# Loads of a tuned attention and feed-forward kernel handed from SyncE to GpSimd

## The chip, the cores and the metric

One core of one Trainium2 chip. The metric is the time of one execution on the device in microseconds (us). Engines: TensorE (PE, its weight loads PEld), VectorE (DVE), ScalarE (ACT), GpSimd (POOL), SyncE (SP, its DMA queue SPq).

Kernels are compared only within the same rounds. With one core there is no other to compare with: a run counts as slow when it is over 1.5% above the fastest run of its kernel in its call.

## The reference

Cut to what matters: a linear attention with decay, computed in blocks along the sequence, then a feed-forward layer with the gate h·cos(h).

```python
# q, k, v: (4, 8, 768, 64) f32; lam: (8,); w_in: (512, 2048); w_out: (2048, 512)
for b in range(nb):                          # blocks of the sequence
    intra = (q_b @ k_b^T * Dmask) @ v_b      # per batch and head
    inter = (q_b * lam_pow) @ kv_state
    out_b = intra + inter
    kv_state = lam_block * kv_state + (k_b * rev_pow)^T @ v_b
x = out.transpose(0, 2, 1, 3).reshape(3072, 512)
h = x @ w_in
return (h * cos(h)) @ w_out
```

## The kernel before

The kernel takes the 3072 tokens as 24 blocks of 128. For each block from number 4 on, q, k and v (256 KB each, f32) are loaded from memory in pieces of 256 bytes, as each head's 64 numbers of one token lie apart.

```python
def start_load(o, x, deps):
    i = nc.sync.dma_start(out=o, in_=x)
    ...
def add_load(n, prio, deps=()):
    b, s0 = n // NB, (n % NB) * P
    for j, (name, src) in enumerate((("q_f", q), ("k_f", k), ("v_f", v))):
        def emit(name=name, src=src):
            t = loads.tile([P, H, D], F32, tag=name, name=name)      # 4 buffers of each
            live[name, n] = t
            return start_load(t, src[b, :, s0:s0 + P, :].transpose([1, 0, 2]), deps)
        issue, load_t[name, n] = dma("SP", 1.2, 0.45, emit, prio + 0.1 * j, deps, get=name)
        issue_t[name, n] = issue
```

GpSimd scales q, casts k and scales v to bf16 (three "preparations"); each frees a load buffer. From block 8 on, q and k are then transposed by a DMA that SyncE issues, and TensorE computes the scores from the result:

```python
a = pl.add("DVE" if n == 0 else "POOL", ..., prep_q, ...)
b = pl.add("ACT" if early else "POOL", 0.61, [load_t["k_f", n], a], prep_k, ...)
d = pl.add("POOL", 1.05, [load_t["v_f", n]], prep_v, ...)
for name, t in (("q_f", a), ("k_f", b), ("v_f", d)):
    issue_t[name, n].frees = [t]
...
if n >= DMA_FROM:                                                # 8
    first_out, T[n] = dma("SP", 1.2, 1.3, transposes_dma, ..., [a, b], get="qkT", ordered=False)
    if n + LAG < NBLK:
        issue_t["q_f", n + LAG].deps.append(first_out)           # loads of n + 2 after transpose n
```

`pl` is a planner that runs before the kernel is built. It gives every task an engine and a **reckoned** duration (the last number but the priority above: 0.45 us for an issue on SyncE, 1.05 for a multiply on GpSimd), plays the whole program through, and fixes the order of instructions on each engine from that. On the chip this order is static: if a task takes longer than was reckoned, the engines behind it wait; they do not take something else first.

Of the kernel before, what the change touches and what calls it, by code (L numbers as in the profile page):

```python
# [10 lines left out]
F32 = mybir.dt.float32  # L11
# [5 lines left out]
QK = 4  # L17
THIRD = 1
SPANS = 2
LAG = 2  # L20
ATT = 1.1
TILES = [4, 2, 3, 4, 4, 4, 3]
# [77 lines left out]
def kernel(  # L100
# [10 lines left out]
    nc = tc.nc  # L111
    B, H, S, D = q.shape
    P = 128
    NB = S // P
    NBLK = B * NB
    NP = H // 2
    DM = H * D
# [93 lines left out]
    def dma(queue, us, issue_us, emit, prio, deps=(), get=None, ordered=True):  # L211
        t = pl.add(queue, issue_us, list(deps) + [last_issue.get(queue) if ordered else None], emit, prio, get=get)
        if ordered:
            last_issue[queue] = t
        d = pl.add("DMA", us, [t], None, prio, lat=1.9)
        d.issue = t
        return t, d

    def start_load(o, x, deps):
        i = nc.sync.dma_start(out=o, in_=x)  # L220
        for d in deps:
            tc.add_manual_dep(i.ins, getattr(d, "issue", d).ins.ins.name, mybir.DependencyInfo(
                mybir.DependencyClass.Sync, mybir.DependencyReason.DATA), reason="order of loads")
        return i
# [9 lines left out]
# [3 lines that stand above are left out]
            def emit(name=name, src=src):  # L237
                t = loads.tile([P, H, D], F32, tag=name, name=name)
                live[name, n] = t
                return start_load(t, src[b, :, s0:s0 + P, :].transpose([1, 0, 2]), deps)  # L240
            issue, load_t[name, n] = dma("SP", 1.2, 0.45, emit, prio + 0.1 * j, deps, get=name)
            issue_t[name, n] = issue

    w_t = {}
# [20 lines left out]
    def add_attention(n):  # L265
# [43 lines left out]
        if n >= DMA_FROM:  # L309
            first_out, T[n] = dma("SP", 1.2, 1.3, transposes_dma, n - LAG + 1.5, [a, b], get="qkT", ordered=False)  # L310
            T[n].lat = 3.0
            ready = [T[n]]
            if n + LAG < NBLK:
                issue_t["q_f", n + LAG].deps.append(first_out)
        else:
            Tq = pl.add("PE", MM(P, 4), [a], lambda: transposes(0), pa(-0.05), get="ps_t")
            T[n] = pl.add("PE", MM(P, 4), [b, Tq], lambda: transposes(1), pa(0.0))
            sides = [slice(0, 1), slice(1, 2)] if early else [slice(0, 2)]
            ready = []
            for x in sides:  # L320
                ready.append(pl.add("DVE", 0.42 if early else 0.7, [T[n] if x.stop == 2 else Tq] + ready,
                                    partial(transposes_out, x), pa(0.0), get=None if ready else "qkT"))
            Tq.frees = [ready[-1]]
            first_out = ready[0]
# [235 lines left out]
    def add_ffn(i):  # L560
        nb, n0 = TILES[i], first[i]
        cols = nb * P
        gate = {}


        third = "ps_f" if i == 0 else "ps_t" if i >= THIRD else "ps_h"

        def bank_of(f):
            return third if f % 3 == 1 else "ps_h"

        for f in range(KF):
            pr = begins[i] + f * unit[i] / KF

            def hidden(f=f):
                t = bank(bank_of(f), [P, 4 * P], F32)
                for kd in range(KD):
                    ins = nc.tensor.matmul(t[:, :cols], lhsT=w_in_sb[:, kd, f * P:(f + 1) * P],  # L577
                                           rhs=live["xT", i][:, kd, :cols], start=(kd == 0), stop=(kd == KD - 1))
                live["h", i, f] = t
                return ins  # L580

            def cosine(f=f):
                c = work.tile([P, 4 * P], F32, tag="cos", name="cos")
                nc.scalar.activation(c[:, :cols], live["h", i, f][:, :cols], AF.Sin, bias=halfpi)  # L584
                live["c", i, f] = c

            def gated(f=f):
                if ("g", i) not in live:
                    live["g", i] = work.tile([P, KF, 4 * P], BF16, tag="g", name="g")
                nc.vector.tensor_mul(live["g", i][:, f, :cols], live.pop(("h", i, f))[:, :cols],  # L590
                                     live.pop(("c", i, f))[:, :cols])

            h = pl.add("PE", MM(cols, 4), [Vo[n] for n in range(n0, n0 + nb)] + [w_t["in", f * WCH // KF]],
                       hidden, pr, get=bank_of(f))
            a = pl.add("ACT", 0.26 + cols * 0.000833, [h], cosine, pr, get="cos")
            d = pl.add("DVE", 0.16 + cols * 0.00104, [a] + ([o_last[i - 2]] if i >= 2 else []), gated, pr)
            h.frees = [d]
            a.frees = [d]
            gate[f] = d
            h_last[i] = hid_t[i, f] = h  # L600
        nxt = unit[i + 1] if i + 1 < len(unit) else unit[i]
        U4 = 4
        for j in range(nb):
            last = n0 + j == NBLK - 1
            tag = ("ps_s", "ps_o", "ps_f", "ps_o")[(nb - 1 - j) % 4] if i == len(TILES) - 1 else "ps_f"

            pieces = [slice(0, DM // 2), slice(DM // 2, DM)] if last else [slice(0, DM)]
            evacs, stores = [], []
            store = None
            for piece, part in enumerate(pieces):  # L610
                width = part.stop - part.start
                for f0 in range(0, KF, U4):
                    pr = begins[i + 1] + (j + f0 / KF) * nxt / nb + piece

                    def project(j=j, f0=f0, tag=tag, piece=piece, part=part):
                        if f0 == 0 and piece == 0:
                            live["f", i, j] = ([bank("ps_s", [P, 2, DM], F32)[:, x, :width] for x in range(2)]
                                               if tag == "ps_s" else [bank(tag, [P, DM], F32)])
                        for f in range(f0, f0 + U4):
                            nc.tensor.matmul(live["f", i, j][piece], lhsT=live["g", i][:, f, j * P:(j + 1) * P],  # L620
                                             rhs=w_out_sb[:, f, part], start=(f == 0), stop=(f == KF - 1))

                    t = pl.add("PE", MM(width, U4), [gate[f] for f in range(f0, f0 + U4)] + [w_t["out", f0 * WCH // KF], store],
                               project, pr, get=tag if f0 == 0 and piece == 0 else None)
                    if f0 == 0 and piece == 0:
                        head = t
                    store = t
                o_last[i] = store

                def project_out(eng, j=j, i=i, piece=piece, width=width):  # L630
                    o = live["o_sb", i, j, piece] = work.tile([P, DM], F32, tag="o_sb", bufs=BUFS["o_sb"], name="o_sb")
                    (nc.scalar.copy if eng == "ACT" else nc.vector.tensor_copy)(o[:, :width], live["f", i, j][piece])  # L632

                def store_out(eng, j=j, piece=piece, part=part, width=width):
                    r0 = (n0 + j) * P
                    if n0 + j < 2 * SPANS:
                        for s, h in enumerate(halves):
                            nc.sync.dma_start(out=out[r0 + s:r0 + P:2, :], in_=live["o_sb", i, j, piece][h])
                        return
                    (nc.scalar if eng == "ACT" else nc.sync).dma_start(  # L640
                        out=out[r0:r0 + P, part], in_=live["o_sb", i, j, piece][:, :width])

                eng, queue = ("DVE", "SP") if last and piece == 0 else ("ACT", "ACT" if last else "SP")
                e = pl.add(eng, 0.12 + width / 1060.0, [store], partial(project_out, eng), begins[i + 1] + (j + 1) * nxt / nb,
                           get="o_sb")
                d = dma(queue, 0.7, 0.4, partial(store_out, queue), n0 + j + 8, [e], ordered=False)[1]
                e.frees = [d]
                evacs.append(e)
            head.frees = evacs

    kept = []
    for j, (name, x) in enumerate((("q", 0), ("k", 0), ("q", 1), ("k", 1), ("v", 0), ("v", 1))):
# [23 lines left out]
    idle_ps = bank("ps_h", [P, 4 * P], F32)  # L676

    def keep_awake(us, at):
        for _ in range(int(us / (4 * P / (1200.0 if at < 5.0 else 2400.0) + 0.0025))):
            nc.tensor.matmul(idle_ps, lhsT=ident, rhs=blank, start=True, stop=True)  # L680

    now = 1.6
    for t in pl.order():
# [35 lines left out]
```

## Time and profile before

| | before |
|---|---|
| time, median of the runs first given | 218.74 us (218.53 to 222.54, 3 runs) |
| span of the profiled run, granted clock | 217.3 us, 0.998 |
| TensorE busy | 95% |
| TensorE waiting for transposed q and k | 1.9 us, once |
| GpSimd busy | 66.2 us (30%) |
| transposes, issue to landing, median | 4.1 us |

Two more parts of the page are needed for the comparison: the slices of GpSimd and of the clock granted to TensorE (each digit is one fortieth of the span, in tenths), and the DMA queues (packets, MB, share of the 16 engines' time; the first is SyncE's, the second GpSimd's).

```profile
POOL 4594003786344545454444441300000000000000
PEclk9999999999999999999999999999999999999999
...
q1 hardware_dynamic: 89200, 29.24, 58.8%
q0 software_dynamic: 4224, 4.19, 11.8%
```

GpSimd is about 45% busy while the loads run, and the clock is full throughout. GpSimd issues only the eight weight loads: 4224 packets, 528 each.

### The profile page before, as it was taken

Reading aid. Unit: us, or ns where it says so; the run is one execution under the profiler, and the core shown is the slowest. Engines: PE = TensorE matmul, PEld = TensorE weight load, DVE = VectorE, ACT = ScalarE, POOL = GpSimd, SP = SyncE. Lnnn points to the kernel's source line nnn. Section 1 sums busy time; section 2 is a strip of 40 time slices with the busy share of each in tenths; the row PEclk is TensorE's granted clock in tenths of the full one; section 3 lists DMA queues with packets and bytes.
Section 4 is the critical chain, followed back from the end, with each engine's and each line's share of the span. In section 5 each row is a group of like instructions: output and inputs, shape, how many; then the busy total and the mean of one; then the engine's idle time right before and its main releaser. Section 6 shows DMA issues by size and latency. Waiting matters only on the chain.

```text
span 217.3 us, 4365 instructions
## 1 busy us (share of the span) xinstructions
PE 206.5 (95%) x1731; PEld 107.9 (50%) x1731; DVE 122.3 (56%) x217; ACT 106.7 (49%) x182; POOL 66.2 (30%) x85
## 2 busy tenths in 40 slices
PE   7797999999996999999999999999999999999993
PEld 2454444557664555454554445455454445555452
DVE  2694776456778677767765574674546334343200
ACT  5782775125664566464545435435444454445320
POOL 4594003786344545454444441300000000000000
PEclk9999999999999999999999999999999999999999
DMA  5999999999899999999899997201001101111112
GB/s 146 347 226 206 194 206 228 238 251 238 190 202 208 224 181 268 183 240 250 180 262 223 210 243 196 69 28 51 39 9 48 51 0 48 48 51 48 48 74 72
DMA packets 93588, 33.84 MB, mean 156 GB/s; under 512 B 80128, under 2 KB 90624, under 8 KB 93568
## 3 DMA queue, kind: packets, MB, share of 16 engines
q1 hardware_dynamic: 89200, 29.24, 58.8%
q0 software_dynamic: 4224, 4.19, 11.8%
q8 instruction: 13, 0.21, 0.4%
q10 hardware_dynamic: 144, 0.13, 0.2%
q14 instruction: 7, 0.06, 0.1%
HBM read 27.27 MB, written 6.29 MB: 154 GB/s over the span
## 4 chain that ended last, share of the span: by engine, by line
PE 89%; DMA 3%; DVE 3%; ACT 2%; issue 1%; POOL 1%; ACTq 0%
PE ps_f L620 36%; PE ps_h L577 26%; PE ps_t L577 10%; PE ps_s L331 3%; PE ps_o L356 3%; PE ps_o L360 2%; PE ps_f L577 2%; DMA qkT<-qk 2%; PE ps_s L620 2%; PE ps_o L620 2%; DVE s_m_sp L469 2%; DMA lam_bc<-in_lam_dram 1%; PE ps_h L680 1%; PE ps_kv L344 1%; POOL q_sp L432 1%
## 5 line engine op out<-in xcount | busy, mean ns | idle before, releaser
L620 PE MATMUL ps_f<-w_out_sb,g 128*128 128x512 bf16 x352 | 88.7, 379 | 0.3 <-ACT o_sb L632 0.2
L590 DVE TENSOR_TENSOR g<-ps_h,cos 128x512 bf16<-128x512 f32 (+2 forms) x77 | 47.2, 614 | 46.2 <-ACT cos L584 45.6
L584 ACT ACTIVATE cos<-ps_h,halfpi 128x512 f32<-128x512 f32 (+2 forms) x77 | 48.2, 626 | 49.4 <-PE ps_h L577 47.4
L577 PE MATMUL ps_h<-xT,w_in_sb 128*128 128x512 bf16 (+2 forms) x308 | 68.0, 349 | 0.0
L577 PEld LDWEIGHTS <-w_in_sb 128*128 128x128 bf16 x448 | 42.9, 98 | 41.4 <-issue 0.7
L620 PEld LDWEIGHTS <-g 128*128 128x128 bf16 x400 | 38.0, 98 | 39.6 <-issue 1.3
L274 POOL TENSOR_TENSOR qk<-q_f,q_scale 128x512 bf16<-128x512 f32 x20 | 20.8, 1042 | 51.8 <-DMA q_f<-in_q_dram 38.2
L584 ACT ACTIVATE cos<-ps_t,halfpi 128x512 f32<-128x512 f32 (+2 forms) x30 | 18.5, 616 | 20.6 <-PE ps_t L577 17.9
L338 DVE TENSOR_TENSOR s_m<-ps_s,mask 128x512 bf16<-128x512 f32 x40 | 26.2, 686 | 3.9 <-PE ps_s L331 3.5
L590 DVE TENSOR_TENSOR g<-ps_t,cos 128x512 bf16<-128x512 f32 (+2 forms) x30 | 18.0, 601 | 16.2 <-ACT cos L584 15.6
L577 PE MATMUL ps_t<-xT,w_in_sb 128*128 128x512 bf16 (+2 forms) x120 | 26.6, 344 | 0.0
L282 POOL TENSOR_TENSOR v_s<-v_f,v_scale 128x512 bf16<-128x512 f32 x20 | 20.8, 1042 | 11.5 <-DMA v_f<-in_v_dram 9.3
L632 ACT COPY o_sb<-ps_f 128x512 f32<-128x512 f32 x22 | 12.9, 585 | 20.1 <-PE ps_f L620 19.9
L350 DVE CAST kv_bd<-ps_kv 64x256 bf16<-64x256 f32 x32 | 13.4, 419 | 2.5 <-PE ps_kv L344 1.9
L278 POOL CAST qk<-k_f 128x512 bf16<-128x512 f32 x20 | 12.2, 609 | 2.8 <-DMA k_f<-in_k_dram 2.8
L366 ACT CAST xT<-ps_o 128x512 bf16<-128x512 f32 x20 | 11.6, 581 | 2.4 <-PE ps_o L360 2.3
L680 PE MATMUL ps_h<-blank,ident 128*128 128x512 bf16 x31 | 9.6, 441 | 1.6 <-POOL ident masks.py:199 1.6
L331 PE MATMUL ps_s<-qkT 64*128 64x128 bf16 x160 | 7.9, 219 | 1.9 <-DMA qkT<-qk 1.9
L360 PE MATMUL ps_o<-s_m,v_s 128*64 128x128 bf16 x160 | 7.9, 220 | 0.0
L356 PEld LDWEIGHTS <-kv_bd 128*64 128x64 bf16 x136 | 4.3, 109 | 6.7 <-issue 5.5
L356 PE MATMUL ps_o<-qkT,kv_bd 128*64 128x128 bf16 x136 | 7.0, 225 | 0.0
L331 PEld LDWEIGHTS <-qkT 64*128 64x128 bf16 x160 | 4.5, 94 | 3.4 <-DMA qkT<-qk 2.0
(88 smaller groups left out, 104.7 us busy)
## 6 DMA issues: line engine op xcount, KB each, us to landing
q_f<-in_q_dram SPq DMA_DIRECT2D x20, 256.0 KB, 3.9
k_f<-in_k_dram SPq DMA_DIRECT2D x20, 256.0 KB, 4.2
v_f<-in_v_dram SPq DMA_DIRECT2D x20, 256.0 KB, 4.4
out_dram<-o_sb SPq DMA_DIRECT2D x19, 256.0 KB, 2.0
w_in_sb<-in_moe_w_in_dram POOLq DMA_DIRECT2D x4, 512.0 KB, 8.0
w_out_sb<-in_moe_w_out_dram POOLq DMA_DIRECT2D x4, 512.0 KB, 14.1
out_dram<-o_sb SPq DMA_DIRECT2D x9, 128.0 KB, 2.7
q_f_sp<-in_q_dram SPq DMA_DIRECT2D x2, 512.0 KB, 5.1
```

The costliest lines, as they stand in the source:

```text
L274: (nc.vector if n == 0 else nc.gpsimd).tensor_mul(live["qk", n][:, 0], live.pop(("q_f", n)), q_scale[:, c, :].unsqueeze(2).to_broadcast([P ...
L282: nc.gpsimd.tensor_mul(live["v_s", n], live.pop(("v_f", n)), v_scale[:, c, :].unsqueeze(2).to_broadcast([P, H, D]))
L331: nc.tensor.matmul(t[:, i, p, :], lhsT=live["qkT", n][h, 1, p, :], rhs=live["qkT", n][h, 0, p, :], start=True, stop=True)
L338: nc.vector.tensor_mul(live["s_m", n][:, i], live["s", n][:, i], mask.unsqueeze(1).to_broadcast([P, NP, P]))
L350: (nc.scalar.copy if early else nc.vector.tensor_copy)(kv_bd[n % NK][h, :, h], kv_ps[h])
L356: nc.tensor.matmul(t[h, p, :], lhsT=kv_bd[(n - 1) % NK][:, p, h], rhs=live["qkT", n][:, 0, p, :], start=(p == 0), stop=False, skip_group_c ...
L360: nc.tensor.matmul(t[h, p, :], lhsT=live["v_s", n][:, 2 * p + i, :], rhs=live["s_m", n][:, i, p, :], start=(p == 0 and c == 0), stop=True, ...
L577: ins = nc.tensor.matmul(t[:, :cols], lhsT=w_in_sb[:, kd, f * P:(f + 1) * P], rhs=live["xT", i][:, kd, :cols], start=(kd == 0), stop=(kd = ...
L584: nc.scalar.activation(c[:, :cols], live["h", i, f][:, :cols], AF.Sin, bias=halfpi)
L590: nc.vector.tensor_mul(live["g", i][:, f, :cols], live.pop(("h", i, f))[:, :cols], live.pop(("c", i, f))[:, :cols])
L620: nc.tensor.matmul(live["f", i, j][piece], lhsT=live["g", i][:, f, j * P:(j + 1) * P], rhs=w_out_sb[:, f, part], start=(f == 0), stop=(f = ...
L632: (nc.scalar.copy if eng == "ACT" else nc.vector.tensor_copy)(o[:, :width], live["f", i, j][piece])
```

## The change

Its intent: SyncE issues loads, transposes and stores in one line, and a transpose that is ready can stand behind loads. GpSimd is less than half busy and can issue DMAs too. So the loads of blocks 10 to 23 go to GpSimd, and SyncE is left with transposes and stores. Two small parts come with it: the second half of the last block's output gets a bank of PSUM (the memory that TensorE writes to) of its own, so that it need not wait for the copy of the first half, and the warm-up matmuls at the start become 41 short ones in place of 10 long ones. The moved loads also lose a rule of order: before, the loads of block n + 2 went out only after the transpose of block n; on GpSimd each load follows the preparation that frees its buffer, four blocks ahead.

```diff
+POOL_FROM = 10
 ...
-    def start_load(o, x, deps):
-        i = nc.sync.dma_start(out=o, in_=x)
+    def start_load(o, x, deps, queue=nc.sync):
+        i = queue.dma_start(out=o, in_=x)
 ...
-                return start_load(t, src[b, :, s0:s0 + P, :].transpose([1, 0, 2]), deps)
-            issue, load_t[name, n] = dma("SP", 1.2, 0.45, emit, prio + 0.1 * j, deps, get=name)
+                return start_load(t, src[b, :, s0:s0 + P, :].transpose([1, 0, 2]), deps,
+                                  nc.gpsimd if n >= POOL_FROM else nc.sync)
+            issue, load_t[name, n] = dma(*(("POOL", 1.2, 0.8) if n >= POOL_FROM else ("SP", 1.2, 0.45)), emit, prio + 0.1 * j,
+                                            deps + [issue_t.get((name, n - 1))], get=name)
 ...
-            if n + LAG < NBLK:
+            if n + LAG < min(NBLK, POOL_FROM):
                 issue_t["q_f", n + LAG].deps.append(first_out)
 ... (last block: the second half of the output)
+                        elif f0 == 0:
+                            live["f", i, j].append(bank("ps_t", [P, DM], F32))
 ... (warm-up)
-        for _ in range(int(us / (4 * P / (1200.0 if at < 5.0 else 2400.0) + 0.0025))):
-            nc.tensor.matmul(idle_ps, lhsT=ident, rhs=blank, start=True, stop=True)
+        cols = P if at < 5.0 else 4 * P
+        for _ in range(int(us / (cols / (1200.0 if at < 5.0 else 2400.0) + 0.0025))):
+            nc.tensor.matmul(idle_ps[:, :cols], lhsT=ident, rhs=blank[:, :cols], start=True, stop=True)
```

The planner reckons 0.8 us for a load issued by GpSimd.

More of the change, by code (lines that the diff above doesn't have):

```diff
@@ L607, in add_ffn @@
             pieces = [slice(0, DM // 2), slice(DM // 2, DM)] if last else [slice(0, DM)]
-            evacs, stores = [], []
             store = None
@@ L613, in add_ffn, with project @@
                     pr = begins[i + 1] + (j + f0 / KF) * nxt / nb + piece
-                    def project(j=j, f0=f0, tag=tag, piece=piece, part=part):
+                    def project(j=j, f0=f0, tag=tag, piece=piece, part=part, width=width):
                         if f0 == 0 and piece == 0:
-                            live["f", i, j] = ([bank("ps_s", [P, 2, DM], F32)[:, x, :width] for x in range(2)]
-                                               if tag == "ps_s" else [bank(tag, [P, DM], F32)])
+                            live["f", i, j] = [bank("ps_s", [P, 2, DM], F32)[:, 0] if tag == "ps_s" else bank(tag, [P, DM], F32)]
+                        elif f0 == 0:
+                            live["f", i, j].append(bank("ps_t", [P, DM], F32))
                         for f in range(f0, f0 + U4):
-                            nc.tensor.matmul(live["f", i, j][piece], lhsT=live["g", i][:, f, j * P:(j + 1) * P],
+                            nc.tensor.matmul(live["f", i, j][piece][:, :width], lhsT=live["g", i][:, f, j * P:(j + 1) * P],
                                              rhs=w_out_sb[:, f, part], start=(f == 0), stop=(f == KF - 1))
                     t = pl.add("PE", MM(width, U4), [gate[f] for f in range(f0, f0 + U4)] + [w_t["out", f0 * WCH // KF], store],
-                               project, pr, get=tag if f0 == 0 and piece == 0 else None)
-                    if f0 == 0 and piece == 0:
+                               project, pr, get=None if f0 else "ps_t" if piece else tag)
+                    if f0 == 0:
                         head = t
@@ L631, in project_out @@
                     o = live["o_sb", i, j, piece] = work.tile([P, DM], F32, tag="o_sb", bufs=BUFS["o_sb"], name="o_sb")
-                    (nc.scalar.copy if eng == "ACT" else nc.vector.tensor_copy)(o[:, :width], live["f", i, j][piece])
+                    (nc.scalar.copy if eng == "ACT" else nc.vector.tensor_copy)(o[:, :width], live["f", i, j][piece][:, :width])
                 def store_out(eng, j=j, piece=piece, part=part, width=width):
@@ L647, in add_ffn @@
                 e.frees = [d]
-                evacs.append(e)
-            head.frees = evacs
+                head.frees = [e]
     kept = []
```

## The prediction

> **What bounds the kernel now.** I read the page first (busy shares, then the 40 slices), then the chain of work that ended last, then the waits of TensorE, then the timelines of TensorE, GpSimd and the SyncE queue in the stretch where the slices show a dip, and the stage table by windows.
>
> ```profile
> span 217.3 us, 4365 instructions
> PE 206.5 (95%) x1731; PEld 107.9 (50%) x1731; DVE 122.3 (56%) x217; ACT 106.7 (49%) x182; POOL 66.2 (30%) x85
> PE   7797999999996999999999999999999999999993
> DMA  5999999999899999999899997201001101111112
> ```
>
> Each digit is the busy share of one slice of 5.4 us. TensorE is full except in the first four slices (start-up), in the 13th (65 to 71 us) and in the last. The DMA engines are full until about 135 us and nearly idle afterwards: the loads run ahead of TensorE and finish early. So supply can matter only in the first 135 us; where it does is in TensorE's waits:
>
> ```profile
> PE ps_s L331 <- DMA qkT<-qk: 1.9, 1, 1.9
> PE ps_h L680 <- POOL ident masks.py:199: 1.6, 1, 1.6
> PE ps_s L494 <- issue: 1.1, 1, 1.1
> PE ps_t L443 <- DVE q_sp L432: 0.8, 1, 0.8
> PE ps_s L620 <- DVE o_sb L632: 0.5, 1, 0.5
> ```
>
> Columns: total us, times, longest. All but the first and the last are start-up. After the first feed-forward matmul (21.2 us) TensorE loses 1.9 us once, at the scores of block 10 (they start at 70.65), 0.5 us near the end, and 0.2 us at an output copy. The stage table agrees: 32.87 us busy of the 35.00 between 36 and 71 us, 38.95 of 39.00 from 71 to 110, 61.00 of 61.00 from 142 to 203. The kernel is bound by TensorE, with about 2.6 us of idleness that a change of the supply or the tail could take away.
>
> Where the 1.9 us come from is in the SyncE queue's timeline (start us, us):
>
> ```profile
> 59.60 2.02 SPq L306 DMA_TRANSPOSE qkT<-qk  x1
> 61.72 1.17 SPq L638 DMA_DIRECT2D out_dram<-o_sb  x2
> 62.94 1.76 SPq L220 DMA_DIRECT2D q_f<-in_q_dram  x1
> 64.74 0.58 SPq L220 DMA_DIRECT2D k_f<-in_k_dram  x1
> 65.37 1.00 SPq L220 DMA_DIRECT2D v_f<-in_v_dram  x1
> 66.53 2.06 SPq L306 DMA_TRANSPOSE qkT<-qk  x1
> ```
>
> The queue is issuing without a gap. Block 10's q and k were ready on GpSimd at 62.15 us, but the transpose waited in line behind 3.3 us of load issues (1.76 + 0.58 + 1.00) and went out at 66.53. It landed 4.1 us later, at 70.6, when TensorE went on; TensorE had been free from about 68.75.
>
> **What the Trainium skill says.** (1) "DMA: Bandwidth & Descriptors", section "Issuing engines are not separate DMA queues": all issuers run on the same 16 DMA engines, and spreading only saves the sequencer's issue time. Here that issue time is what the transpose waited for, so the move can help; but the DMA share is 0.98 between 36 and 71 us, so bandwidth is not gained. (2) Same page, "Queues, rings and completion order": an engine takes turns between queue rows, packet by packet. So transposes on SyncE's row should no longer stand behind all queued loads; no trace of before shows this. (3) "Perfetto Trace Analysis", section "DMA Instruction — SWDGE (GPSIMD)": the GpSimd's profiled time of a DMA is descriptor generation, not data. The trace agrees: the weight loads take 0.75 to 0.94 us on GpSimd and land after 5.6 to 16.9 us. (4) "SBUF — State Buffer", section "SBUF: two separate sides": some VectorE operations lock GpSimd out of a shared port, and descriptors with it. The trace shows one case at start-up: a GpSimd multiply that takes 1.04 us elsewhere took 1.54 beside a VectorE multiply with SBUF inputs. From 35 us on the same operation is 1.04 everywhere, because VectorE then reads PSUM; I expect no lock-out.
>
> **The change part by part.**
>
> *Loads of blocks 10 to 23: 14 x 3 = 42 DMA issues leave SyncE for GpSimd.* Off SyncE: 0.57 us (undisturbed) to 1.8 us each, about 2.5 us a block. SyncE keeps transposes (1.24 us at least, median 1.86) and stores. The static order shows the GpSimd program as multiply q, load q, copy k, load k, multiply v, load v, from block 6 on; each load fills the buffer just freed, four blocks ahead. Block 10's loads then go out near 44 us, against 57.2 now.
>
> *What GpSimd pays.* Per block now 1.04 + 0.61 + 1.04 = 2.7 us. A load adds an issue x, plus perhaps 0.1 us to wait for its own previous instruction (my guess). The only durations are those of the weight loads: 0.75 to 0.94 us, 528 packets each. A block load has twice the pieces (128 x 8 runs of 256 bytes). If the cost is mainly fixed, x is about 0.8; if it follows the pieces, up to 1.5. With x = 0.8 the cycle is c = 2.65 + 2.4 + 0.3 = 5.3 us; with 1.0, 5.9; with 1.2, 6.5.
>
> *What TensorE demands.* In the trace the scores of block 8 start at 61.66 and of block 16 at 104.59. The new order puts 2.6 us of feed-forward matmuls (four groups of four with 256 columns, 0.43 us each, and one of four with 512, 0.86) ahead of block 8, and takes them from later. With the 1.9 us wait gone, block 8 is wanted near 64.3, 13 near 87, 16 near 102.7. Afterwards a block is wanted only every 7 to 8 us.
>
> *Supply against demand (estimate).* Block 6's preparation starts at 42.66 as now. Block n is transposed and landed at 42.66 + (n - 6)c + 2.6 (q, one load, k) + 4.1 (the median from issue to landing). For block 10: 49.4 + 4 x 5.3 = 70.6, wanted near 74: no wait. For 13: 86.5 against 87; for 16: 102.4 against 102.7. So x = 0.8 just fits, and each further 0.1 us of x makes the last of these later by 10 x 0.3 = 3 us. Transposes that land sooner than 4.1 us, their ring now free of loads, buy back about one such step.
>
> *Second half of the last block in its own bank.* It removes TensorE's 0.52 us wait for VectorE's copy at 212.3. That wait lies on the path to the end: -0.5 us.
>
> *Warm-up matmuls, 41 of 128 columns in place of 10 of 512.* The ten take 3.92 us, end at 5.54, and the first useful matmul waits for VectorE until 6.30. 41 at a quarter of 0.43 us are as long. Worth 0.
>
> *Rest.* Same matmuls, the same start-up order on every engine; only middle groups change places, and TensorE is full there.
>
> Sum if x is near 0.8: -1.9 - 0.5 - about 0.1 = -2.5 at best, with a few tenths given back at blocks 13 and 16: 218.7 - 2.2 = 216.5 us.
>
> **The rivals.**
> (A) *GpSimd becomes the supply's bound.* For: the balance above has no slack; twice the pieces of a weight load. Against: the planner in the kernel reckons 0.8 us for such an issue, as it reckons 0.45 for SyncE where the trace shows 0.57, so it may have been measured; the page of the skill puts most of a small DMA's cost in fixed parts. At x = 0.9 about 2 us of waits (218.5 us); at 1.0 some 5 (221); at 1.2 over 10 (above 226).
> (B) *Transfers stay the bound.* The DMA engines are full anyway; block 10's loads from 44 us on share them with those of 8 and 9. For: share 0.98. Against: blocks 8 and 9 now land at about 48 and 53 to 55 us, while GpSimd would take them only near 53 and 58; a delay of 2 us is hidden. If it is not, 1 to 2 us come back: 217.5 to 218.5.
> (C) *The wait just moves*, from block 10's transpose to another block's or to a store that waits behind a transpose on SyncE: same time, 218 to 219 us.
>
> **Range and chances.** I give about half the weight to x near 0.8 (216 to 217 us), a quarter to B, C or x near 0.9 (217.5 to 219.5), and a quarter to a clear GpSimd bound (220 and more). The middle of that is 217.2 us; 8 in 10 between 215.8 and 223.5. Faster by over 2% would be below 214.4: the idleness that the change touches sums to 2.6 us, so 0.03. Slower by over 2% is above 223.1 and needs x of about 1.1 or more: 0.17. Within 2%: 0.80.
>
> **What would show it.** Right: the groups by line show 42 load issues on GpSimd near 0.8 us; the wait of the scores for the transpose is gone from TensorE's waits, the 13th slice is 9; the last block's wait on VectorE is gone; the start-up is unchanged at about 21.2 us. Wrong: load issues of 1.0 us or more, and TensorE waiting for the transposes of blocks 9 to 16 with GpSimd solid before them; or GpSimd waiting for loads that it issued long before (B).

## The result, and the profile after

After: 229.45 us median (229.39 to 231.48, 4 runs); before, in the same rounds: 218.72 (218.53 to 222.54, 4 runs). The ratio is 1.0525, with a 95% interval of 1.0468 to 1.0582: slower by 5%, outside the predicted range. A ratio here is the mean time of one kernel's fast runs over that of the other's fast runs of the same rounds, so it is not quite the ratio of the medians. Both profiled runs are fast: spans of 217.3 us at a clock of 0.998 before and 229.6 us at 0.982 after, 12.3 us more. The profiled run of the change was the longest of its four (231.48 us; the other three have spans of 227.7 us), so these 12.3 us are about 2 us more than in its other runs.

The page of the kernel after, lines as before:

```profile
span 229.6 us, 4422 instructions
...
PE 208.1 (91%) x1734; PEld 111.9 (49%) x1762; DVE 123.0 (54%) x217; ACT 106.8 (46%) x182; POOL 105.6 (46%) x127
...
PE   7899999999939979499589999999999999999993
...
POOL 4692006888888888888888894300000000000000
PEclk9999999999999999799979999999999999999998
...
q1 hardware_dynamic: 45520, 18.23, 32.8%
q0 software_dynamic: 7584, 15.21, 29.4%
```

TensorE has the same work (208.1 us busy against 206.5) but four dips (slices 12, 15, 17 and 20) where it had one. Two of them are followed by a clock of 0.7. GpSimd stands at 8 in every slice from the 8th to the 23rd: at 80 to 90% without a break, which makes it a candidate for what sets the pace. The queues show something that was not asked about: the 42 loads cost SyncE's queue 43,680 packets (1040 each) and cost GpSimd's queue 3,360 (80 each) for the same bytes.

TensorE's waits (total us, times, longest) and GpSimd's waits for its own instructions:

```profile
PE ps_s L334 <- DMA qkT<-qk: 11.4, 4, 3.5
```

```profile
POOL v_f L221 <- POOL v_s L285: 4.8, 14, 0.7
POOL q_f L221 <- POOL qk L277: 4.5, 14, 0.6
POOL k_f L221 <- POOL qk L281: 4.5, 14, 0.6
```

The wait for transposed q and k did not vanish; it grew from 1.9 to 11.4 us. And GpSimd waits 13.8 us in all, once before each of its 42 load issues, for *its own* preparation to complete. One cycle of GpSimd's timeline (start us, duration us; in brackets the idle time before it and what ended it) shows how:

```profile
48.26 1.06 POOL L277 TENSOR_TENSOR qk<-q_f,q_scale 128x512 bf16<-128x512 f32 x1
49.61 0.93 POOL L221 DMA_DIRECT2D q_f<-in_q_dram  x1 [0.30 <-POOL qk L277]
50.53 0.62 POOL L281 CAST qk<-k_f 128x512 bf16<-128x512 f32 x1
51.46 0.88 POOL L221 DMA_DIRECT2D k_f<-in_k_dram  x1 [0.30 <-POOL qk L281]
52.36 1.06 POOL L285 TENSOR_TENSOR v_s<-v_f,v_scale 128x512 bf16<-128x512 f32 x1
53.71 0.93 POOL L221 DMA_DIRECT2D v_f<-in_v_dram  x1 [0.30 <-POOL v_s L285]
54.66 1.06 POOL L277 TENSOR_TENSOR qk<-q_f,q_scale 128x512 bf16<-128x512 f32 x1
```

From one q multiply to the next: 54.66 − 48.26 = 6.40 us. That is 2.74 us of preparation, 2.74 us of issues (0.91 each) and 0.90 us of waits (0.30 each): 1.22 us for each load. The load refills the buffer that the instruction right before it has read, so it must wait until that instruction has completed, and GpSimd stands still meanwhile.

TensorE's timeline, the scores that waited for a transpose (blocks 8, 11, 13 and 16):

```profile
66.00 0.40 PE L334 MATMUL ps_s<-qkT 64*128 64x128 bf16 x8 [2.72 <-DMA qkT<-qk]
...
81.83 0.40 PE L334 MATMUL ps_s<-qkT 64*128 64x128 bf16 x8 [1.81 <-DMA qkT<-qk]
...
94.78 0.55 PE L334 MATMUL ps_s<-qkT 64*128 64x128 bf16 x8 [3.40 <-DMA qkT<-qk]
...
115.42 0.61 PE L334 MATMUL ps_s<-qkT 64*128 64x128 bf16 x8 [3.47 <-DMA qkT<-qk]
```

The scores of block 16 start at 115.42 us, against 104.59 before: 10.8 us later. The same feed-forward work lies ahead of them in both kernels (352 weight loads in each trace). After that no block waits. The line of the kernel before:

```profile
104.59 0.40 PE L331 MATMUL ps_s<-qkT 64*128 64x128 bf16 x8
```

In the change, the scores of blocks 13 and 16 took 0.55 and 0.61 us in place of 0.40; the stage table says why (columns: stretch in us, its length, busy time and instructions of each engine, granted clock, DMA share, GB/s):

```profile
94.70:97.00 2.30, 2.22 (x13) 0.92 (x14) 1.29 (x2) 0.00 (x0) 1.71 (x4) 0.54 0.48 119
97.00:98.00 1.00, 1.00 (x4) 0.40 (x3) 0.00 (x0) 0.00 (x0) 0.98 (x2) 0.50 0.62 209
...
115.40:117.40 2.00, 1.98 (x12) 0.94 (x13) 0.69 (x1) 0.00 (x0) 1.69 (x4) 0.50 0.45 121
```

After each of these two waits TensorE is granted half its clock for about 3.4 us, and so loses about 1.7 us more (half of 3.4, an estimate). The first of these losses lies before a later wait, so it is hidden by it; the second is not.

**The sum**: +10.8 (block 16's scores) + 1.7 (the second slow stretch) − 0.5 (the wait on VectorE near the end, which is gone) = +12.0 of the 12.3 us.

### The profile page after: what moved, and what is told of

Read it like the earlier page. It is cut to its first block, busy times and chain, and to the rows that moved or that the text cites.

```text
span 229.6 us, 4422 instructions
## 1 busy us (share of the span) xinstructions
PE 208.1 (91%) x1734; PEld 111.9 (49%) x1762; DVE 123.0 (54%) x217; ACT 106.8 (46%) x182; POOL 105.6 (46%) x127
## 4 chain that ended last, share of the span: by engine, by line
PE 48%; issue 17%; POOL 17%; DMA 13%; SPq 3%; ACT 0%; POOLq 0%; ACTq 0%
PE ps_f L623 21%; PE ps_h L580 14%; DMA w_out_sb<-in_moe_w_out_dram 7%; PE ps_t L580 6%; POOL qk L277 5%; POOL v_s L285 5%; POOL qk L281 3%; SPq L221 3%; DMA k_f_sp<-in_k_dram 3%; DMA qkT<-qk 2%; DMA v_f<-in_v_dram 2%; PE ps_o L623 2%; PE ps_s L334 1%; POOL w_in_sb L253 1%; PE ps_o L359 1%
## 5 line engine op out<-in xcount | busy, mean ns | idle before, releaser
L623 PE MATMUL ps_f<-w_out_sb,g 128*128 128x512 bf16 x331 | 86.3, 384 | 2.6 <-issue 1.3
L580 PEld LDWEIGHTS <-w_in_sb 128*128 128x128 bf16 x448 | 43.5, 99 | 42.9 <-issue 3.0
L334 PE MATMUL ps_s<-qkT 64*128 64x128 bf16 x160 | 8.3, 226 | 11.4 <-DMA qkT<-qk 11.4
L221 POOL DMA_DIRECT2D v_f<-in_v_dram x14 | 13.0, 926 | 4.8 <-POOL v_s L285 4.8
L221 POOL DMA_DIRECT2D q_f<-in_q_dram x14 | 13.0, 928 | 4.5 <-POOL qk L277 4.5
L221 POOL DMA_DIRECT2D k_f<-in_k_dram x14 | 12.4, 884 | 4.5 <-POOL qk L281 4.5
L683 PE MATMUL ps_h<-blank,ident 128*128 128x128 bf16 (+1 forms) x58 | 9.4, 333 | 1.8 <-POOL ident masks.py:199 1.6
```

The costliest lines, as they stand in the source:

```text
L221: i = queue.dma_start(out=o, in_=x)
L334: nc.tensor.matmul(t[:, i, p, :], lhsT=live["qkT", n][h, 1, p, :], rhs=live["qkT", n][h, 0, p, :], start=True, stop=True)
L580: ins = nc.tensor.matmul(t[:, :cols], lhsT=w_in_sb[:, kd, f * P:(f + 1) * P], rhs=live["xT", i][:, kd, :cols], start=(kd == 0), stop=(kd = ...
L623: nc.tensor.matmul(live["f", i, j][piece][:, :width], lhsT=live["g", i][:, f, j * P:(j + 1) * P], rhs=w_out_sb[:, f, part], start=(f == 0) ...
```

## The experiments

The theory: GpSimd's own pace, 6.40 us a block where the prediction put 5.3 and the planner 5.1, makes the transposed blocks late. Rivals: the transfers themselves (GpSimd's big packets crowd the DMA engines that transposes and SyncE's loads share); the small parts; and the halved clock as a cause rather than a result. A fourth question is whether the slow pace as such costs the time, or that the static order was laid out for a faster one. All edits below are to the changed kernel, and every kernel gave correct results.

**1. The small parts alone.**

```diff
-POOL_FROM = 10
+POOL_FROM = 99
```

> The change without its main part: all loads stay on SyncE; only the bank of the last block's second half and the narrower warm-up matmuls are as in the changed kernel. Both theories (GpSimd's pace, or sharing of the DMA engines by two queues) put the whole loss on the moved loads, so this should be the kernel before less 0.5 us: 218.2 us, no slower than 218.8. If it is at 220 or more, the small parts do harm and the loss has a second source.

Measured: 220.28 us (12 runs) against 220.47 (15 runs), ratio 1.0006 (0.9975 to 1.0037). TensorE's wait on VectorE near the end is gone from the profile, but its 0.5 us cannot be told from the noise in the time. TensorE waits 3.3 us for transposes in this kernel, in three places. The small parts are not where the loss comes from.

**2. GpSimd made busy, with no DMA moved.** Experiment 1 plus two idle GpSimd instructions after each preparation of blocks 6 to 19:

```diff
+    def ballast(n):
+        if 6 <= n < 20:
+            nc.gpsimd.tensor_mul(idle_a, blank, blank)
+            nc.gpsimd.memset(idle_b, 0.0)
 ... (called at the end of prep_q, prep_k and prep_v)
```

> As e1, loads all on SyncE, but GpSimd runs an idle multiply and a memset after each of its three preparations of blocks 6 to 19 (the results are not used), to bring its cycle from 2.7 to about 6.4 us a block as in the changed kernel, without any DMA moved. Theory 1 (GpSimd's pace alone): TensorE waits for transposes as in the changed kernel, 226 to 232 us. Theory 2 (the second DMA queue slows transposes or loads): the pace does not matter, 218 to 220 us.

Measured: the cycle came out at 6.94 us, more than aimed at; 232.14 us, ratio 1.0542 (1.0489 to 1.0596), TensorE waits 12.2 us for transposes, in five places. A busy GpSimd alone can cost as much as the change, with all loads on SyncE. But as the cycle overshot, this does not yet say whether 6.4 us would.

**3. Three smaller ballasts**, to read the loss against the cycle. The first has only the multiply, on 472 of the 512 columns; the others keep it whole and fill fewer columns:

```diff
-            nc.gpsimd.memset(idle_b, 0.0)
+            nc.gpsimd.memset(idle_b[:, :160], 0.0)      # or :344
```

> The small parts alone, no DMA moved, and one idle GpSimd multiply of 472 columns after each preparation of blocks 6 to 19, sized for a cycle of 5.3 us, the one that the prediction reckoned with. The earlier ballast, at 6.93 us, gave 1.054. Theory (the balance of supply and demand was right, and only the cycle put into it was wrong): 5.3 us fits, so the time is that of the small parts alone, ratio 0.995 to 1.006, and TensorE waits for transposes no more than 4 us. Rival (the balance itself was too kind to the change): a loss already here, 1.010 or more.

> As before, with a multiply of 512 columns and a fill of 160, sized for a cycle of 5.9 us. Theory: block 16's preparation starts near 41.8 + 59 = 100.8, its transpose lands near 108, some 3 us after it is wanted in the kernel before: ratio 1.010 to 1.025 (the prediction had 221 us for x = 1.0, 1.010). Rival: already close to the full loss, above 1.035, or none at all.

> As before, with a fill of 344 columns, sized for the cycle that the change shows, 6.4 to 6.5 us. Theory (GpSimd's pace alone is the loss): 1.042 to 1.056 of the kernel before, as the change has 1.0525. Rival (the load packets and the shared DMA engines add their own part): 1.03 or less.

Measured, with the fourth row from experiment 2 and the fifth from the change itself. The cycle is the mean over ten blocks (nine in the fourth row), from the q multiply of block 6 on. For the change it is (106.88 − 41.84) / 10; it is over 6.40 as three of its ten cycles lasted some 0.3 us longer.

| | cycle, us | ratio to before | 95% interval | waits for transposes, us | transposes to landing, median us |
|---|---|---|---|---|---|
| ballast, small | 5.35 | 1.0028 | 1.0005 to 1.0050 | 3.3 in 2 | 3.5 |
| ballast, middle | 6.06 | 1.0239 | 1.0172 to 1.0305 | 6.5 in 3 | 2.8 |
| ballast, large | 6.52 | 1.0389 | 1.0344 to 1.0433 | 8.6 in 4 | 2.8 |
| ballast of experiment 2 | 6.94 | 1.0542 | 1.0489 to 1.0596 | 12.2 in 5 | 2.8 |
| the change | 6.50 | 1.0525 | 1.0468 to 1.0582 | 11.4 in 4 | 4.6 |

At 5.35 us there is hardly a loss, and TensorE waits no longer for transposes than in experiment 1, so at the cycle that the prediction had put in, the pace by itself did fit. From there each further microsecond of cycle costs 6.5 to 8.0 us from row to row (for example (1.0542 − 1.0239) × 220 / (6.94 − 6.06) = 7.6). At the change's own pace the ballast costs 3.9%, and the change 5.25%. The expectation (1.042 to 1.056) was missed on the low side, as was the rival's (1.03 or less): **the pace alone costs about three quarters as much as the change**, and some 1.4%, 3 us, need something more. (The ballast kernels have the static order of experiment 1. It asks for block 8 after 180 feed-forward weight loads, the change after 200; for block 16 both ask after the same 352.) The two profiles show where these 3 us are:

```profile
PE ps_s L345 <- DMA qkT<-qk: 8.6, 4, 3.6
...
qkT<-qk SPq DMA_TRANSPOSE x16, 2.8
```

```profile
qkT<-qk SPq DMA_TRANSPOSE x16, 4.6
```

(The first fence is the large ballast, its waits and its DMA issues, whose last number is the median time to landing; the second is the change.) In the ballast kernel block 16's transpose goes out at 110.64 us, later than the change's at 109.81, and yet its scores start at 114.06 without waiting:

```profile
110.64 1.24 SPq L320 DMA_TRANSPOSE qkT<-qk  x1
...
114.06 0.40 PE L345 MATMUL ps_s<-qkT 64*128 64x128 bf16 x8
```

In the change the transpose takes 5.6 us to land (2.8 in the ballast kernel), the scores wait 3.47 us until 115.42, and that wait is the one that brings the unhidden slow clock. That is 1.4 us before the scores and 1.7 after them, of the 3.5 us between the two spans (226.1 and 229.6). So in these two traces the transposes' slower landing beside GpSimd's loads is the second part. This is read from one profiled run of each kernel; no experiment isolates it, nor why they land slower. The kernel before, with all loads on SyncE at a faster pace, had 4.1 us.

**4. The change with a true cost in the planner.**

```diff
-("POOL", 1.2, 0.8)
+("POOL", 1.2, 1.25)
```

> The changed kernel, but the planner that lays out the static order reckons 1.25 us for a load issue on GpSimd (0.92 plus a 0.30 wait, as measured) in place of 0.80. GpSimd's cycle stays at 6.4 us. Theory 1a (GpSimd's rate itself is too low for the kernel): still 225 us or more. Theory 1b (the rate would do, but TensorE's static order was laid out for a supply every 5.1 us, so it meets each block too early): TensorE's waits for transposes shrink from 11.4 to under 3 us, the clock stays up, 216 to 220 us.

Measured: 222.75 us against 220.47, ratio 1.0148 (1.0059 to 1.0236, wide, but far from 1.05). GpSimd's pace is unchanged (6.49 us a block over the same ten), and so are its waits for itself (13.8 us). Block 16's scores start even later, at 117.63, but without a wait: the planner put other matmuls before them (400 feed-forward weight loads lie ahead in place of 352). TensorE waits 3.1 us, in two places, and the clock is 1.000. The time missed its expectation (216 to 220 us) on the high side, and lies nearer to theory 1b than to 1a. This answers the fourth question: **the slow pace costs little where the order knows of it**. Most of the loss is a static order laid out for 0.8 us a load, met by 1.22.

**5. Each GpSimd load one preparation later**, so that the buffer that it refills was read by the instruction before the previous one (the planner's issue cost is 0.95 here):

```diff
-        for name, t in (("q_f", a), ("k_f", b), ("v_f", d)):
+        for name, t in (("q_f", a), ("k_f", b), ("v_f", d)) if n + 4 < POOL_FROM else (("q_f", b), ("k_f", d), ("v_f", d)):
             issue_t[name, n].frees = [t]
+        if n + 3 >= POOL_FROM and ("v_f", n - 1) in issue_t:
+            issue_t["v_f", n - 1].frees = [a]
```

> The changed kernel with each GpSimd load issued one preparation later (load q after copy k, load k after multiply v, load v after the next multiply q), so that it need not wait for the instruction just before it, and with 0.95 us in the planner. If the 0.30 us before each load is that wait for the preparation's own completion, it vanishes and the cycle falls from 6.4 to about 5.5 us: 216 to 219 us. If it is a fixed cost of a load issue, the cycle stays near 6.4 and the time at 224 us or more.

Measured: 222.84 us against 220.47, ratio 1.0112 (1.0060 to 1.0164). GpSimd's timeline in this kernel:

```profile
52.10 0.92 POOL L221 DMA_DIRECT2D k_f<-in_k_dram  x1
53.05 1.06 POOL L277 TENSOR_TENSOR qk<-q_f,q_scale 128x512 bf16<-128x512 f32 x1
54.03 0.92 POOL L221 DMA_DIRECT2D v_f<-in_v_dram  x1
54.95 0.62 POOL L281 CAST qk<-k_f 128x512 bf16<-128x512 f32 x1
```

No bracket stands behind a load: the 0.30 us waits are gone to the last one, and the cycle is 5.29 us. The mechanism came as expected, the time (216 to 219 us) did not: still 1.1% are missing, where the small ballast at nearly the same cycle lost 0.3%. The intervals of experiments 4 and 5 overlap, and the planner's cost differs from the change's here too, so what the shorter cycle saves beyond the planner's number is not shown. TensorE waits once, 3.94 us, at the scores of block 8, whose transpose SyncE issued only at 61.05 us (55.81 in the kernel before). Ahead of it in SyncE's line stood one load issue of 3.06 us and stores; the same kind of issue took 0.57 us undisturbed. GpSimd's first loads are in flight at that time, four blocks ahead of their use.

**6. The loads all on SyncE, but the wait of block 10 removed by order alone.** Experiment 1 plus one edit: the loads of block 11 go out after the transpose of block 10.

```diff
             if n + LAG < min(NBLK, POOL_FROM):
                 issue_t["q_f", n + LAG].deps.append(first_out)
+            if n == 10:
+                issue_t["q_f", n + 1].deps.append(first_out)
```

> Loads all on SyncE as in e1; one edit: the load of block 11 is issued after the transpose of block 10 and no longer ahead of it. If the 1.9 us wait of the kernel before is just the line in front of that transpose, it shrinks to under 0.5 us with nothing moved to GpSimd: 1.9 us less than e1, ratio to before near 0.990. If the wait only moves to another block (the load comes 2 us later), ratio 0.998 to 1.002.

Measured: 216.27 us (6 runs) against 219.02 (11), ratio 0.9886 (0.9848 to 0.9924): the fastest version found, and faster than both kernels. TensorE's timeline has two small waits for transposes left, none at block 10:

```profile
81.32 0.40 PE L336 MATMUL ps_s<-qkT 64*128 64x128 bf16 x8 [0.94 <-DMA qkT<-qk]
...
103.27 0.40 PE L336 MATMUL ps_s<-qkT 64*128 64x128 bf16 x8 [0.32 <-DMA qkT<-qk]
```

The interval lies below 1. So the 1.9 us of the kernel before did come from the line in SyncE's queue, and another engine was not needed to win them.

**7. Loads from block 12 on, one preparation later, with the swap.** `POOL_FROM = 12`, and the edits of experiments 5 and 6 together, meant to keep GpSimd's loads out of the crowded stretch.

> As e5 (each GpSimd load one preparation later, 0.95 us in the planner), but only the loads from block 12 on move, so that GpSimd puts nothing on the DMA engines before about 53 us, while SyncE is still loading blocks 8 and 9; and load 11 after transpose 10 as in e6. Theory: what was left in e5 (a 3.9 us wait at 67.5 us) comes from GpSimd's early loads competing with SyncE's loads of blocks 8 and 9 between 43 and 57 us. Then that wait is gone and the ratio to before is 0.985 to 0.995. Rival: transposes on a queue beside GpSimd's are slower anyway, then waits of 2 to 4 us stay and the ratio is 1.00 to 1.01.

Measured: 229.88 us (6 runs, 223.8 to 238.6, four of them slow) against 219.02; the two fast runs alone give 1.0255 (1.0207 to 1.0304). It missed its aim: the edits bunched eight GpSimd loads between 62.9 and 71 us. The profiled run is a slow one, so its waits are only described: the transpose of block 10, issued at 64.67 us, landed 8.9 us later, SyncE's two last load issues took 3.11 and 4.24 us, and TensorE waited:

```profile
73.60 0.61 PE L338 MATMUL ps_s<-qkT 64*128 64x128 bf16 x8 [5.29 <-DMA qkT<-qk]
```

It is a sign that GpSimd's loads hold up SyncE's transfers when they come in a burst, but no more than that, as it stands in a slow run alone.

**8. The change with the clock kept up.** Six idle matmuls of 512 columns ahead of the scores of blocks 13 and 16:

```diff
+            for _ in range(6 if n in (13, 16) else 0):
+                nc.tensor.matmul(t[:, 0], lhsT=ident, rhs=blank, start=True, stop=True)
```

> The changed kernel with six idle matmuls of 512 columns ahead of the scores of blocks 13 and 16, in the two waits of 3.4 us after which the granted clock fell to half for about 3.4 us. They cost nothing while TensorE would wait anyway (6 x 0.22 = 1.3 us of 3.4). If the lower clock is part of the loss, it goes: mean clock from 0.982 to 1.00 and about 3.4 us less than the changed kernel, ratio to before near 1.036 in place of 1.0525. If the clock is only a sign, the ratio stays above 1.05.

Measured: 229.23 us (4 runs) against 219.02, ratio 1.0469 (1.0440 to 1.0499), beside 1.0525 for the change: about 0.6%, 1.2 us, was saved, not 3.4, and as the two intervals overlap, even that is not clear of noise. The clock rose from 0.982 to 0.992: the slow stretches at blocks 13 and 16 are gone, but a new one, at 0.51 from 66.4 to 69.9 us, follows the wait at block 8, so the test is not a clean one. Block 16's scores start at 114.55 (115.42 in the change): faster matmuls in between only met the next late block sooner. The halved clock is a consequence that costs some 1 us here, not the cause.

**9. Experiment 5 with each load two blocks ahead of its use in place of four**, to spread them and keep them away from block 8:

```diff
+        for name, m, t in (("q_f", n + 2, b), ("k_f", n + 2, d), ("v_f", n + 1, a)):
+            if POOL_FROM <= m < NBLK:
+                issue_t[name, m].deps.append(t)
```

> e7 missed its aim: its edit bunched eight GpSimd loads at 63 to 71 us. Here e5 (all loads from block 10 on GpSimd, one preparation later, cycle 5.3 us) with one edit: each load runs two blocks ahead of its use and not four, so the first goes out near 52 us and not at 43, evenly spaced. Theory: the 3.9 us wait left in e5 came from early GpSimd loads crowding SyncE's loads of blocks 8 and 9; then transpose 8 goes out near 56 us as in the kernel before, that wait is under 1 us and the ratio to before falls from 1.011 to 0.985 to 0.998. Rival: transposes beside GpSimd's loads land late anyway; then waits of over 2 us stay and the ratio is 1.00 or more.

Measured: 219.86 us (22 runs) against 221.10 (43), ratio 0.9909 (0.9872 to 0.9945). From 1.0112 to 0.9909 by sending the same loads later, as expected if early crowding was the remaining cost of experiment 5. Two things hold this back. Ten of the 22 runs count as slow (8 of 43 for the kernel before), and over all runs the mean is 0.999 of that of the kernel before. And the profiled run is a slow one; it still waits 4.8 us at block 8, so that the crowding is gone is not shown.

**10. The swap, and GpSimd's loads only from block 16 on.** `POOL_FROM = 16` with the edits of experiments 6 and 9.

> e6 (load 11 after transpose 10, all else on SyncE) but loads from block 16 on GpSimd in the form of e9, where TensorE wants a block only every 7 to 8 us. Theory: GpSimd's pace of 5.3 us is no bound there, and SyncE's line is none either, so the move is worth nothing: as e6, ratio to before 0.985 to 0.992. If moving loads helps transposes even there, below 0.985; if it hurts by sharing, above 0.995.

Measured: 219.49 us (22 runs) against 221.10, ratio 0.9924 (0.9892 to 0.9957); 4 of the 22 runs count as slow, the profiled one among them. Its interval overlaps those of experiments 6 and 9. So with its costs dealt with, the handing over to GpSimd reaches at best, in its fast runs, about what one edit of the order on SyncE reaches, and adds nothing to it.

## Why the prediction was wrong

- **What bounds the kernel, and where the wait is: right.** Block 10's wait was the line on SyncE (experiment 6 won it back and gave 1.1%).
- **"What GpSimd pays": the step that failed.** The prediction put the cycle at c = 2.65 + 2.4 + 0.3 = 5.3 us. Measured: 6.40 us in an undisturbed cycle, 6.50 on average. Term by term: the issue 0.91 in place of 0.80, three times, +0.33; the wait for its own instruction 0.30 in place of the guess of 0.1, three times, +0.6; preparations 2.74 in place of 2.65, +0.1. (Its own durations, 1.04 + 0.61 + 1.04, add up to 2.69, and with 2.4 and 0.3 to 5.39, not 5.3. Over ten cycles that is 0.9 us, three times the 0.3 us of slack that it found at block 16.) The issue turned out nearly fixed, as the prediction favoured (0.91 us for a load of 1024 pieces, within the 0.75 to 0.94 of the weight loads). The largest error was the guess of 0.1, which no view of the kernel before showed.
- **"Supply against demand": right in form, and steep as it said.** It had put block 16 on the chip at 102.4 us; it landed at 115.4. The miss of 13.0 us: the start −0.8 (41.84 for 42.66), ten cycles +12.0, q and k ready 2.9 us into the cycle in place of 2.6 (+0.3), landing 5.6 us for 4.1 (+1.5). The ballasts confirm "x = 0.8 just fits" for the pace alone (5.35 us: 1.003) and show a slope of 6.5 to 8.0 us for each us of cycle; the prediction had 10 for the last block's supply. For 5.9 us it gave 221 us, +1.0%; between the ballasts at 5.35 and 6.06 one reads 1.019 there, so the balance was somewhat kind. A right c would not have been enough either: experiment 5 ran at 5.29 us with the loads on GpSimd and still lost 1.1%.
- **Transposes that land sooner: wrong.** The prediction hoped that their queue, free of loads, would beat 4.1 us. They took 4.6, against 2.8 in the ballast kernel of equal pace with all loads on SyncE. By the two traces that is the second part of the loss (about 3 us of 12).
- **Not in the prediction: the halved clock** after the long waits, some 1 us by experiment 8 (not clear of noise) and 1.7 by the profile.
- **Tail and warm-up: right in the profile but for one point.** The wait on VectorE is gone, and the first transposes start at 6.28 us (6.30 before). The first feed-forward matmul, for which it gave 21.2 us, came at 20.15, as a wait of 1.1 us in the profile before is missing after. None of this can be seen in the time (experiment 1).
- **Rival A was the true one, but by another way.** The issue itself took 0.91 us, not the 1.0 or more that was to be its sign, and for x = 0.9 the prediction had 218.5 us. Only with the wait added (1.22 in all) is the cycle that of x = 1.2, for which it had "above 226"; measured were 229.45. Rival A had a chance of 0.17 where the argument against it rested on the planner's 0.8, "it may have been measured". That number was the fault: with 1.25 there, the same loads cost 1.5% (0.6 to 2.4) in place of 5%. **Rival B** showed as well, in another form: not a delay of all transfers but of transposes and of the transfers of SyncE near 60 us. Experiment 5 points to it; 7 and 9 fit it, but only slow runs of them were profiled.
- **Chances.** A balance without slack whose slope is 3 us for each 0.1 us of an unmeasured term does not bear a chance of 0.80 for "within 2%".

**Open:** why transposes land slower beside GpSimd's loads. The bigger packets and the shared engines are consistent with it, but no run changed the packets alone. Open too is why experiments 7 and 9 scatter more than the others (4 of 6 and 10 of 22 runs slow).

## What to carry to other kernels

Before an idle engine is given a stream's DMA issues, add up its whole cycle: the issue itself and the wait for its own last instruction if the DMA refills what that instruction has just read, which one instruction of distance removes. Where a planner fixes the order, put measured costs into it first: here that number alone was worth about 3.7%. And when one transfer stands in line behind others, try the order within the line first; it won 1.1% here with one edit, as much as the best form of the move in its fast runs.

## What the Trainium skill lacked or had wrong

- **"DMA: Bandwidth & Descriptors", section "Anatomy of one DMA — SWDGE (gpsimd) path"**, calls descriptor generation "small, variable". The skill says elsewhere that GpSimd's cores do it, and this page gives about 1 us to the first byte of such a DMA; but for how long one load keeps GpSimd from other work was found on no page: 0.88 to 0.93 us here for 256 KB in 1024 pieces, on an engine whose multiply takes 1.06.
- **Found on no page:** a GpSimd load that refills the buffer of GpSimd's previous instruction waits 0.30 us for it with the engine idle (42 times, 13.8 us in all with some longer ones); with one instruction in between the wait is gone (experiment 5).
- **"DMA: Bandwidth & Descriptors", section "Issuing engines are not separate DMA queues"**, says that another issuer saves only the sequencer's time. The runs agree that nothing more is gained, but the move is not neutral: the same loads went from 1040 packets each to 80, and transposes took 4.6 us in place of 2.8 at an equal pace of GpSimd (4.1 in the kernel before), and 8.9 us in a burst of eight loads, in a slow run.
- **"TensorE: Matmul & The Clock Gate", section "What's actually happening"**, states that the clock halves after an idle window of about 3.4 us, which runs free. Waits of 3.40 and 3.47 us were followed by a clock of 0.50 to 0.54 for some 3.4 us, which agrees. But a wait need not be so long: in the large ballast kernel one of 2.43 us was followed by 3.4 us at 0.50 (95.2 to 98.6 us), while one of 2.72 in the change was not.
